# The order of keys, values and queries in the second layer's first blocks (linear attention and a Mish MLP, two layers, one core)

## The chip, the cores and the metric

One core of one Trainium2 chip runs the whole program in one launch. The metric is device time in microseconds (us). Engines: TensorE (PE in the profile, its weight loads PEld), VectorE (DVE), ScalarE (ACT), GpSimd (POOL), and SyncE (SP), which issues every data transfer (DMA) of this kernel.

## The reference

x has 2048 rows of 640. Two sublayers, A and B, alternate, each behind a layer norm and with a residual; the pair is run twice with the same weights.

```
x = x + A(layernorm(x)); x = x + B(layernorm(x)); x = x + A(layernorm(x)); x = x + B(layernorm(x))

A: q, k, v = split(x @ wqkv) into 32 heads of 20
   pq = q @ w_phi[h];  pk = k @ w_phi[h]
   phi = concat(softmax(p), softmax(-p))          # 40 features a head, for q and for k
   kv = phi_k^T v;  z = sum of phi_k over the rows
   o = (phi_q kv) / (phi_q z + 1e-6);  return o @ wo
B: h = x @ w1 + b1;  return (h * tanh(softplus(h))) @ w2      # 640 -> 1536 -> 640
```

All is float32. The products of A's keys with its values run over all 2048 rows before any query can be answered.

## The kernel before

**Precision.** Each float32 operand of a large product is kept as a high and a low part in a faster matmul type, and a product is three matmuls (high x high, high x low, low x high). So a projection of 128 rows to 640 columns is 2 halves x 5 chunks of the depth x 3 = 30 matmuls of 128x320 (`project_half`, L344).

**Stages of a layer.** `attend_first` projects keys, values and queries and sums keys times values; `attend_second` answers the queries and applies wo; `dense` is B. Rows go in 8 blocks of 256, each two tiles of 128 rows. The matmuls of B's second product are L733, of its first L691.

**`attend_first`.** For each block there are six units, a letter and a tile number: k0, k1, v0, v1, q0, q1. A unit is a projection (30 matmuls), an eviction by ScalarE (`act`, L116) and, for keys and queries, the feature chain in `features`: two reductions (L368), two subtractions (L369 and L371; for queries L369 is on POOL), an exponential on ScalarE, a sum (L377), a reciprocal (L378) and a scaling on POOL (L379). Keys then multiply their values into one accumulator, kva (L416, 32 small matmuls a tile). Queries are transposed on VectorE (L424) and stored (L428). Units are generators: `pending` holds the running ones, and `advance` moves each a step on after every new unit's projection has been recorded.

The projections read the block's rows as transposed chunks, xth (high) and xtl (low, made on VectorE, L286): two chunks of 128x512 and one of 128x256. In the second layer the rows of the next block are loaded already transposed (L325), and its chunks are made while the present block is recorded (`nxt.step()`).

**On-chip accumulators.** Projections use the "mm" ring (two tiles of two banks). The values of block 0 use the "one" ring instead (four banks, L436), which also holds kva (one bank, from its memset L484 to the stage's end) and B's first product. While B's last contraction still holds both "mm" tiles, the values of block 0 can already run.

**Weights.** In the first layer the queries' and keys' weights are folded with w_phi and spilled to `wp_d`. In the second they come back: `load_q_weights` (L179, ten loads of 320 KB into the "r2" buffers, which held B's second weights), `load_k_weights` (L185, ten into "r1", which held B's first weights). The values' weights are loaded raw (L126) and split by ScalarE (L127) and VectorE (L128) in `load_v_weights`, inside `dense`. wo's rows are loaded (L141) and split by ScalarE (L148) and POOL (L149) after block 1 has been recorded (`load_o_weights`).

**What sets the order.** The stage stands in a block whose instructions a scheduler orders by the readiness that it estimates; the recorded order decides between instructions that are ready together. ScalarE's `act` operations keep the recorded order. Only `attend_second`'s TensorE and SP orders are written by hand.

Of the kernel before, what the change touches and what calls it, by code (L numbers as in the profile page):

```python
# [41 lines left out]
def kernel(  # L42
# [118 lines left out]
    def r2_pair(j):  # L161
        if j >= 10:
            w = r2_wide(j)
            return w[:, 0], w[:, 1]
        return tuple(wts.tile([P, D], F32R, tag=f"r2{s}{j}", name=f"r2{s}{j}") for s in "hl")
# [9 lines left out]
    def load_q_weights():  # L175
        ws = [r2_pair(k) for k in range(KD)]
        for k in range(KD):
            for s in range(2):
                nc.sync.dma_start(ws[k][s].bitcast(F32), wp_d[0, s, k])  # L179
        return ws  # L180

    def load_k_weights(kv_ws):
        for k in range(KD):
            for s in range(2):
                nc.sync.dma_start(kv_ws[k][s][:, :D].bitcast(F32), wp_d[1, s, k])  # L185
# [69 lines left out]
    def norm_scale(b, mvs):  # L255

        ve = work.tile([P, BT], F32, tag="ve", name="ve", bufs=2)
        for t in range(BT):
            nc.gpsimd.tensor_scalar(ve[:, t:t + 1], mvs[t][:, 1:2], LN_EPS, 1.0, op0=ALU.add, op1=ALU.mult)
        nc.gpsimd.tensor_tensor(stats[:, b, 0], ve, neg_half, op=ALU.pow)  # L260
        for t in range(BT):
            nc.vector.scalar_tensor_tensor(stats[:, b, 1, t:t + 1], mvs[t][:, 0:1], -1.0,
                                           stats[:, b, 0, t:t + 1], op0=ALU.mult, op1=ALU.mult)
# [55 lines left out]
    def load_turned(src, tiles):  # L319

        cols = []
        for c, make in zip(range(0, KD, 2), tiles):
            n = min(2, KD - c)
            cols.append(make()[:, :n * BLK].rearrange("p (k s) -> p k s", k=n))
            nc.sync.dma_start(cols[-1], src[c * P:(c + n) * P].rearrange("(k p) s -> p k s", p=P))  # L325
        return Transposed(cols=cols)
# [55 lines left out]
    def fetch(x_src, b, xt=None):  # L382
        xt = x_tile() if xt is None else xt
        nc.sync.dma_start(xt, row_block(x_src, b))
        return xt

    def attend_first(layer, x_src, first):


        def fetch_normed(b):  # L390
            if layer:
                return load_turned(n2_d[b], [row_tile] * 3)
            xt = fetch(x_src, b)
            norm_scale(b, [norm_stats(t, xt) for t in range(BT)])
            return xt

        pending = []

        def advance():
            for g in pending[::-1]:  # L400
                try:
                    next(g)
                except StopIteration:
                    pending.remove(g)

        def keys(xts, i, v):
            e = big_tile()
            yield from features(project(xts, i % BT, kv_ws, 0), e, False)
            yield
            if i % BT == 0 and BT < i < NT - BT:  # L410
                yield
            for r in range(9):
                for j in range(4):
                    h = 3 * (4 * (r // 3) + j) + r % 3
                    if h < H:
                        nc.tensor.matmul(kva[32 * j:32 * j + DH + 1, 40 * r:40 * r + 40],  # L416
                                         v[:, (DH + 1) * h:(DH + 1) * (h + 1)], e[:, 40 * h:40 * h + 40],
                                         start=(i == 0 and r == 0), stop=(i == NT - 1), skip_group_check=True)

        def queries(xts, i, ps=None):  # L420
            e = query_tile(i)
            yield from features(project(xts, i % BT, q_ws, 0) if ps is None else ps, e, True)

            nc.vector.transpose(e, e)  # L424
            b, t = divmod(i, BT)
            dst = e_d[b].rearrange("(j f) (t q s) -> t q f j s", f=32, t=BT, s=32)
            for q in range(4):
                nc.sync.dma_start(dst[t, q], e[32 * q:32 * q + 32].rearrange("f (j s) -> f j s", s=32))  # L428
                if b == NB - 1:
                    yield  # L430

        def values(xts, i, v):
            vv = v.rearrange("p (h d) -> p h d", d=DH + 1)
            act(vv[:, :, DH], ident[:, :H], AF.Copy, scale=0.0, bias=1.0)
            if i < BT:
                pv = project(xts, i, kv_ws, D, [one_tile(), one_tile()])  # L436
                for c in range(2):
                    act(vv[:, c * H // 2:(c + 1) * H // 2, :DH],
                        pv[c][:, :HC].rearrange("p (h d) -> p h d", d=DH), AF.Copy)
            else:  # L440
                pv = project(xts, i % BT, kv_ws, D)
                act(vv[:, :, :DH].rearrange("p (c h) d -> p c h d", c=2),
                    both(pv).rearrange("p c (h d) -> p c h d", d=DH), AF.Copy)
            yield

        if first is None:
            with tc.manual_schedule(engines={mybir.EngineType.SP}):
                bd = big_tile()[:120, :720].rearrange("p (t c) -> p t c", t=6)
                nc.sync.dma_start(bd[:, :3], phi_bd[:, :3])
                raw = load_raw(0, range(3))  # L450
                xt = fetch_normed(0)
                nc.sync.dma_start(bd[:, 3:], phi_bd[:, 3:])
                raw += load_raw(0, range(3, 6))
                nxt = normed(0, xt).all()
                q_ws = [r2_pair(k) for k in range(KD)]
                fold_phi(q_ws, bd, raw)
                kv_ws = load_v_weights()
                raw = load_raw(1)
            nc.sync.dma_start(mask, bass.AP(tensor=head_mask.tensor, offset=head_mask.offset,
                                            ap=[[1, 120], [120 * (DH + 1), 3]]))  # L460
        else:
            nxt, kv_ws = first
            q_ws = load_q_weights()
        for b in range(NB):
            xts = nxt
            order = ("k0", "k1", "v0", "v1", "q0", "q1")
            if b == 0:
                order = ("v0", "q0", "v1", "k0", "q1", "k1")
            elif b == 1:
                order = ("k0", "q0", "k1", "v0", "q1", "v1")  # L470
            elif b == NB - 1:
                order = ("k0", "k1", "v0", "v1", "q0")
            vs = [v_tile() for _ in range(BT)]
            for n, (kind, t) in enumerate(order):
                t = int(t)
                i = b * BT + t
                if b == 0 and n == 1:
                    if layer:
                        load_k_weights(kv_ws)
                if b == 0 and n == 3:  # L480
                    if layer == 0:
                        fold_phi(kv_ws, bd, raw)
                    kva = one_tile()
                    nc.vector.memset(kva[:, :360], 0.0)  # L484
                if b == NB - 1 and n == 3:
                    loaded = {0: load(0)}
                if b + 1 < NB:
                    if n == 0:
                        xt = fetch_normed(b + 1)
                    elif n == 2:  # L490
                        nxt = xt if layer else normed(b + 1, xt)
                    elif n > 2:
                        nxt.step()
                g = {"k": lambda: keys(xts, i, vs[t]), "q": lambda: queries(xts, i),
                     "v": lambda: values(xts, i, vs[t])}[kind]()
                next(g)
                advance()
                pending.append(g)
            if b == 1:
                if layer == 0:  # L500
                    spill_qk_weights(kv_ws, q_ws)
                o_ws = load_o_weights()

        def rest():

            ps = [one_tile(), one_tile()]
            project_half(ps[0], xts, 1, q_ws, 0, 0)
            advance()
            advance()
            yield  # L510
            project_half(ps[1], xts, 1, q_ws, 0, 1, range(3))
            yield
            project_half(ps[1], xts, 1, q_ws, 0, 1, range(3, KD))
            pending.append(queries(xts, NT - 1, ps))
            next(pending[-1])
            while pending:
                yield
                advance()

        return kva, o_ws, loaded, rest()  # L520
# [374 lines left out]
```

## Time and profile before

| | us |
|---|---|
| median of 3 runs | 1383.88 (1383.01 to 1385.57) |
| the profiled execution | 1385.02 |
| its span, first to last instruction | 1383.2 |
| second layer's `attend_first` in it | about 702 to 936 |
| TensorE busy | 1364.8 |
| VectorE busy | 1082.0 |
| ScalarE busy | 583.1 |
| POOL busy | 440.5 |

The granted TensorE clock is 0.999 of full speed. A row of the time-ordered view reads: start (us from the span's start), duration, engine, line, operation, what it writes <- what it reads, shapes, count, and in brackets the engine's idle time before it with what ended that. A line's "DMA to landing" row is the time from issue to landing.

### The profile page before, as it was taken

What the parts mean: (1) busy time and instruction counts of PE and PEld (TensorE: products, weight loads), DVE (VectorE), ACT (ScalarE), POOL (GpSimd) and SP (SyncE); (2) the same over time, 40 slices, a digit from 0 to 9 for tenths busy, and PEclk for the clock granted to TensorE, in tenths of its full rate; (3) what the DMA queues carried; (4) which work ended last, traced back from release to release, by engine and by line L of the source; (5) the groups of instructions that cost most, each with busy time, mean ns of one, the idle gap of its engine ahead of it and who ended that gap; (6) DMA issues with size and microseconds to landing.
All of it is one profiled execution on the core that took longest, in us unless ns stands there. A gap on an engine that the chain in (4) does not pass through costs nothing. (4 is left out here: it accounts for less than half of the span.)

```text
span 1383.2 us, 30808 instructions
## 1 busy us (share of the span) xinstructions
PE 1364.8 (99%) x12866; PEld 1351.4 (98%) x12866; DVE 1082.0 (78%) x1820; ACT 583.1 (42%) x971; POOL 440.5 (32%) x334
## 2 busy tenths in 40 slices
PE   8999999999999999999999899999999999999998
PEld 7999999999999999999999899999999999999998
DVE  5799977886698887788769988988678776677775
ACT  4444434222445454545444333432235444444443
POOL 1353543353322222222234434453342111111112
PEclk9999999999999999999999999999999999999999
DMA  8532433779624432344474333458975211333200
GB/s 320 172 73 59 73 50 69 216 228 305 223 66 96 115 97 62 74 113 96 134 249 84 76 63 59 69 115 262 278 260 172 77 45 52 97 96 96 76 21 19
DMA packets 350276, 169.67 MB, mean 123 GB/s; under 512 B 287097, under 2 KB 323689, under 8 KB 350137
## 3 DMA queue, kind: packets, MB, share of 16 engines
q1 hardware_dynamic: 350137, 167.72, 45.0%
q8 instruction: 100, 1.64, 0.5%
q14 instruction: 39, 0.32, 0.1%
HBM read 104.76 MB, written 62.91 MB: 121 GB/s over the span
## 5 line engine op out<-in xcount | busy, mean ns | idle before, releaser
L733 PE MATMUL mm<-r2h,ol 128*128 128x320 f32 x1280 | 305.1, 309 | 0.8 <-ACT ol L716 0.8
L717 POOL TENSOR_TENSOR ol<-big,ol 128x512 fp32r<-128x512 f32 (+1 forms) x98 | 130.0, 1327 | 485.4 <-ACT ol L716 409.1
L691 PE MATMUL one<-xtl,r1h 128*128 128x256 f32 x960 | 268.2, 279 | 0.0
L691 PE MATMUL one<-xth,r1l 128*128 128x256 f32 x960 | 268.0, 279 | 0.0
L691 PE MATMUL one<-xth,r1h 128*128 128x256 f32 x960 | 265.9, 279 | 0.0
L733 PEld LDWEIGHTS mm<-r2h,ol 128*128 128x128 f32 x1280 | 219.1, 188 | 1.3 <-ACT ol L716 1.1
L733 PE MATMUL mm<-r2l,ol 128*128 128x320 f32 x640 | 197.3, 309 | 0.0
L344 PE MATMUL mm<-r1h,xtl 128*128 128x320 f32 x600 | 185.8, 310 | 1.7 <-DVE xtl L286 1.7
L344 PE MATMUL mm<-r1h,xth 128*128 128x320 f32 x600 | 187.4, 312 | 0.0
L344 PE MATMUL mm<-r1l,xth 128*128 128x320 f32 x600 | 186.0, 310 | 0.0
L691 PEld LDWEIGHTS one<-xtl,r1h 128*128 128x128 f32 x960 | 180.4, 188 | 0.0
L691 PEld LDWEIGHTS one<-xth,r1l 128*128 128x128 f32 x960 | 180.4, 188 | 0.0
L691 PEld LDWEIGHTS one<-xth,r1h 128*128 128x128 f32 x960 | 179.6, 188 | 0.0
L706 DVE TENSOR_SCALAR big<-big 128x512 f32<-128x512 f32 (+1 forms) x98 | 57.0, 582 | 109.9 <-ACT big L704 109.7
L379 POOL TENSOR_TENSOR r<-r,r 128x1280 f32<-128x1280 f32 x32 | 75.8, 2370 | 149.4 <-DVE r L378 143.5
L733 PEld LDWEIGHTS mm<-r2l,ol 128*128 128x128 f32 x640 | 120.2, 188 | 0.0
L708 ACT ACTIVATE big<-big,two 128x512 f32<-128x512 f32 (+1 forms) x98 | 70.2, 717 | 116.0 <-DVE big L707 116.0
L704 ACT ACTIVATE big<-one,b1s 128x256 f32<-128x256 f32 x192 | 80.9, 468 | 90.1 <-PE one L691 89.5
L716 ACT ACTIVATE ol<-big 128x512 fp32r<-128x512 f32 (+1 forms) x98 | 61.0, 622 | 136.3 <-DVE big L715 136.2
L344 PEld LDWEIGHTS mm<-r1h,xtl 128*128 128x128 f32 x600 | 112.7, 188 | 2.2 <-DVE xtl L286 2.1
L344 PEld LDWEIGHTS mm<-r1h,xth 128*128 128x128 f32 x600 | 112.7, 188 | 0.7
L344 PEld LDWEIGHTS mm<-r1l,xth 128*128 128x128 f32 x600 | 112.7, 188 | 0.1
(128 smaller groups left out, 3129.8 us busy)
## 6 DMA issues: line engine op xcount, KB each, us to landing
e_d<-r SPq DMA_DIRECT2D x128, 160.0 KB, 4.0
big<-e_d SPq DMA_DIRECT2D x32, 640.0 KB, 7.9
x_d<-xt SPq DMA_DIRECT2D x23, 640.0 KB, 3.7
xt<-x_d SPq DMA_DIRECT2D x22, 640.0 KB, 5.2
n_d<-xn SPq DMA_DIRECT2D x176, 80.0 KB, 2.2
xt<-in_x SPq DMA_DIRECT2D x16, 640.0 KB, 6.6
xn<-x_d SPq DMA_DIRECT2D x28, 320.0 KB, 4.7
v<-n_d SPq DMA_DIRECT2D x30, 256.0 KB, 3.1
```

Of the source, the lines that this page charges most:

```text
L344: nc.tensor.matmul(ps[:, :HC], a[:, sl], r, start=(k == 0 and n == 0), stop=(k == KD - 1 and n == 2))
L379: nc.gpsimd.tensor_tensor(eg, eg, r.unsqueeze(2).to_broadcast([P, 2 * H, DH]), op=ALU.mult)
L691: nc.tensor.matmul(ph[:, j, :], l, r, start=(n == 0), stop=(n == 3 * KD - 1))
L704: exps[0] = nc.scalar.activation(part(ta, 0)[:, j - js.start], ph[:, j, :], AF.Exp, bias=b1s[:, 2 * pr + j:2 * pr + j + 1]).ins
L706: nc.vector.tensor_scalar_min(e, e, E_CAP)
L708: nc.scalar.activation(r, n, AF.Ln, bias=two)
L716: nc.scalar.activation(ah[:, js], n, AF.Copy)
L717: nc.gpsimd.tensor_tensor(al[:, js], n, ah[:, js].bitcast(F32), op=ALU.subtract)
L733: nc.tensor.matmul(pys[t][:, c, :HC], l[:, j, sl], r, start=(f == 0 and n == 0), stop=(f == KF - 1 and n == 2))
```

## The change

```diff
             nxt, kv_ws = first
+            load_k_weights(kv_ws)
             q_ws = load_q_weights()
         for b in range(NB):
             xts = nxt
             order = ("k0", "k1", "v0", "v1", "q0", "q1")
-            if b == 0:
+            if b == 0 and layer:
+                order = ("v0", "k0", "k1", "v1", "q0", "q1")
+            elif b == 0:
                 order = ("v0", "q0", "v1", "k0", "q1", "k1")
-            elif b == 1:
+            elif b == 1 and not layer:
                 order = ("k0", "q0", "k1", "v0", "q1", "v1")
...
-                if b == 0 and n == 1:
-                    if layer:
-                        load_k_weights(kv_ws)
-                if b == 0 and n == 3:
+                if b == 0 and n == (1 if layer else 3):
                     if layer == 0:
                         fold_phi(kv_ws, bd, raw)
                     kva = one_tile()
```

Only the second layer changes. Its block 0 takes v0 k0 k1 v1 q0 q1, its block 1 the order of the later blocks. The ten loads of the keys' weights are recorded ahead of the ten of the queries'; kva is allocated and cleared after one unit of block 0 in place of three.

The two built programs, TensorE's order around the change (matmuls; L733 and values are mixed in the first entry):

```
before  v0 (30) and 20 of v1 among the last L733 | q0 30 | 10 of v1 | k0 30 | q1 30 | k1 30
        block 1: k0 30 | q0 30 | k1 30 | v0 9, L416 32, v0 21 | q1 30 | v1 30
        block 2: L416 64 | k0 30 | k1 30 | L416 32 | v0 30 | v1 30 | q0 30 | q1 30
after   v0 (30) and 15 of v1 among the last L733 | k0 30 | k1 30 | 15 of v1 | q0 30 | q1 30
        block 1: k0 14, L416 10, k0 16 | L416 22 | k1 30 | L416 32 | v0 30 | v1 30 | q0 30 | q1 30
        block 2: L416 32 | k0 30 | L416 32 | k1 30 | v0 30 | v1 30 | q0 30 | q1 30
```

## The prediction

> **What bounds the kernel now.** I read the page's head first, then the busy time by windows, then the waits of TensorE, and last the instructions in order of time around each wait that is left.
>
> ```profile
> span 1383.2 us, 30808 instructions
> PE 1364.8 (99%) x12866; PEld 1351.4 (98%) x12866; DVE 1082.0 (78%) x1820; ACT 583.1 (42%) x971; POOL 440.5 (32%) x334
> ```
>
> TensorE is busy in 99% of the span, and the change neither adds nor removes a matmul. So only TensorE's holes can pay. By windows (us; then the busy time of PE, PEld, DVE, ACT, POOL) two stretches near the start of the second layer have holes:
>
> ```profile
> 700.00:710.00 10.00, 9.17 (x61) 8.67 (x60) 5.40 (x12) 4.20 (x10) 2.64 (x2) 1.00 0.89 336
> 760.00:770.00 10.00, 5.97 (x157) 5.32 (x156) 10.00 (x10) 2.99 (x5) 5.02 (x4) 1.00 0.25 61
> ```
>
> In 760:770 TensorE is idle for 4.03 us while VectorE is full: VectorE bounds that stretch. The waits of TensorE in 690:800 name three causes (total, times, longest):
>
> ```profile
> PE one L416 <- POOL big L379: 2.8, 1, 2.8
> PE mm L344 <- DVE xtl L286: 1.3, 1, 1.3
> PE mm L733 <- ACT ol L716: 0.8, 1, 0.8
> ```
>
> The same by instruction:
>
> ```profile
> 761.14 0.83 PE L416 MATMUL one<-big,v 128*21 128x40 f32 x64
> 764.72 0.83 PE L416 MATMUL one<-big,v 128*21 128x40 f32 x64 [2.75 <-POOL big L379]
> 765.48 0.41 PE L344 MATMUL mm<-r1h,xth 128*128 128x320 f32 x1
> 765.73 0.31 PE L344 MATMUL mm<-r1l,xth 128*128 128x320 f32 x1
> ...
> 767.49 0.31 PE L344 MATMUL mm<-r1l,xth 128*128 128x320 f32 x1
> 769.08 0.42 PE L344 MATMUL mm<-r1h,xtl 128*128 128x320 f32 x1 [1.28 <-DVE xtl L286]
> 769.33 0.31 PE L344 MATMUL mm<-r1h,xth 128*128 128x320 f32 x1
> ```
>
> From 765.73 to 767.49 there are 12 projection matmuls, one per 0.147 us; the 0.31 is a record's length, so an idle time counted from it is too short. By starts: 64 records of L416 take 764.72 to 765.48, 0.76 us, so the second group could have started at 761.90; it started 2.82 us later. The low part at 769.08 could have started at 767.64, was 1.44 late, and restarted 0.10 slow (0.25 to the next). **Together 4.4 us.** The first loss is the wait for the normalised key features of block 1's first tile (L379), the second for block 2's last transposed chunk (L286). Why VectorE is late:
>
> ```profile
> 727.88 0.81 DVE L369 TENSOR_TENSOR big<-big,m 128x640 f32<-128x640 f32 x1
> 758.33 2.99 DVE L369 TENSOR_TENSOR big<-big,m 128x640 f32<-128x640 f32 x1
> 762.38 2.84 DVE L286 TENSOR_TENSOR xtl<-xn,xth 128x512 fp32r<-128x512 f32 x1
> 758.00 2.63 POOL L379 TENSOR_TENSOR big<-big,r 128x1280 f32<-128x1280 f32 x1 [5.83 <-DVE r L378]
> 761.92 2.75 POOL L379 TENSOR_TENSOR big<-big,r 128x1280 f32<-128x1280 f32 x1 [1.29 <-DVE r L378]
> ```
>
> L369 takes 0.81 alone, 2.99 when it meets POOL's L379 (758.00 to 760.63): it ends 0.69 after POOL does. So VectorE is in arrears from the features of blocks 0 and 1 alone, which for keys and queries start all at once.
>
> **The change part by part.**
>
> *Order of the six units.* Block 0 goes from v0 q0 v1 k0 q1 k1 to v0 k0 k1 v1 q0 q1, block 1 from k0 q0 k1 v0 q1 v1 to k0 k1 v0 v1 q0 q1. Each unit is 30 matmuls, and the same 12 units run before block 2. What moves is which feature chains stand first on VectorE. In the new program's VectorE order, block 1's two key chains are finished before block 2's chunks need VectorE, and the two L416 products of block 1 stand after all of block 1's projections, the second behind block 2's first.
>
> I price that by chaining the new order by hand from these rows:
>
> ```profile
> 723.04 1.55 DVE L368 TENSOR_REDUCE m<-r 128x32 f32<-128x640 f32 x2
> 728.61 1.48 DVE L377 TENSOR_REDUCE r<-r 128x64 f32<-128x1280 f32 x1
> 731.34 0.54 DVE L378 RECIPROCAL r<-r 128x64 f32<-128x64 f32 x1
> 723.94 1.28 POOL L369 TENSOR_TENSOR r<-r,m 128x640 f32<-128x640 f32 x1 [2.25 <-DVE m L368]
> 721.68 0.74 ACT L116 ACTIVATE v<-one 128x320 f32<-128x320 f32 x2
> ```
>
> Started back to back, each record but the first overlaps by some 0.08: a pair of L368 costs 1.45, L369 or L371 0.74, L377 1.40, L378 0.46, L286 0.6 (0.34 for the small one).
> - First key tile, from about 723.9: pair, L369, pair, L371, L286, L369, L377, L371, L286, L378 are 8.9, so 732.8; L379 2.37 more: 735.2. TensorE asks for it 14 matmuls into block 1, at about 737. Slack 1.8.
> - Block 1's last chunk: 732.8 + 1.45 + 1.40 = 735.6, where it meets POOL's L369 of the first query tile (735.2 + 1.28 = 736.5), so about 736.8; asked for at 737.1 behind ten L416. Slack 0.3, the smallest.
> - Block 1's first keys: from 736.5 three pairs, six L369/L371, three L377, three L378, a transpose (L424, 1.45), L286: 16.4, and 4 to 5 for meetings with POOL as above: 757.4; L379: 759.8. Asked for at about 762.6. Slack 2.8.
> - Block 1's second keys end near 763.5, asked for near 767.5; block 2's last chunk near 763.9, asked for at 765.4.
>
> So both losses go: **-4.4**, and next late is block 1's last chunk, still in time.
>
> *What the new order costs early.* v0's two banks, kva and v1's first half fill the ring of four "one" banks, so v1's second half can't run beside the last contraction as it does now.
>
> ```profile
> 707.57 0.31 PE L733 MATMUL mm<-r2h,ol 128*128 128x320 f32 x1
> 708.71 0.41 PE L733 MATMUL mm<-r2h,ol 128*128 128x320 f32 x1 [0.83 <-ACT ol L716]
> 709.25 0.31 PE L733 MATMUL mm<-r2l,ol 128*128 128x320 f32 x1
> 709.53 0.56 PE L733 MATMUL mm<-r2h,ol 128*128 128x320 f32 x2
> 708.24 0.42 ACT L716 ACTIVATE ol<-big 128x256 fp32r<-128x256 f32 x1 [1.69 <-DVE big L715]
> 709.08 1.56 ACT L127 ACTIVATE r1h<-v 128x640 fp32r<-128x640 f32 x2 [0.42 <-DMA v<-in_wv]
> ```
>
> Ahead of the wait that ends at 708.71 stand 24 value matmuls now and 18 in the new order. Its end is ScalarE's (708.24 + 0.42), not TensorE's, so the six come later for nothing: 6 x 0.147 = **+0.9**. Then four L733 (to 709.40), and the next three value matmuls need weight chunk 2, which ScalarE copies in half of 1.56 from 709.08, to 709.85: 0.45 and a slow restart 0.10. The little wait at 709.53 (0.13 + 0.10) is covered by that. **+0.3**. Bounds for this last term: -0.2, if the chunk's load is earlier, and 0.6.
>
> *More visits of L416.* Blocks 0 and 1 enter it five times instead of three. The steady chain of work prices a visit:
>
> ```profile
> 800.46 26.60 PE mm L344 x180
> 827.06 1.41 PE one L416 x126
> ```
>
> 180 matmuls at 0.147 are 26.4, shown as 26.60: 0.2 for changing over and back. Two more visits: **+0.4** (0 to 0.4).
>
> *Keys' weights ahead of queries'.* In the built order of SP's queue nothing moves: the ten query loads still stand ahead of the ten key loads, since their buffers come free earlier. The price is zero, but k0 now wants the keys' weights sooner. Key loads:
>
> ```profile
> L185 SPq DMA_DIRECT2D r1l<-wp_d x5: 320/383/629, 694.5 to 701.7; - x5
> DMA to landing us min/median/max: 4.4/6.6/8.0
> ```
>
> The last is issued at 701.7 and lands by 709.7 at the worst; k0 starts near 715. It hides behind the value matmuls with 5 us to spare; without that cover it would cost TensorE's wait one for one.
>
> *The memset of kva and the queries' stores.* L484 (0.36 now at 722.6) moves up to where VectorE waits, -0.3 of its queue, counted in the first chain. The queries' four stores per tile move behind block 3's row loads on SP; they are read back after the last block, so nothing waits for them but the next query tile's eviction (a rival below).
>
> **The sum.** -4.4 + 0.9 + 0.3 + 0.4 = -2.8. The profiled execution took 1385.02 (span 1383.2, 1.8 outside it) and would take 1382.2. It stands 1.1 over the median of 1383.88; against that the forecast is **1381.1**. The bounds of the terms: 4.0 (by windows) to 4.4 gained, 0.7 to 1.9 lost, so 1380.2 to 1381.8.
>
> **A rule of the skill against the change.** L369's 2.99 above against 0.81 is a meeting with POOL. The Trainium skill, "SBUF — State Buffer", section "SBUF: two separate sides", has a VectorE instruction with two inputs from SBUF and a GpSimd instruction share one pair of ports, exclusively, for the whole instruction. By that rule the new order isn't safe where a chunk follows a reciprocal that has just released L379; its result is the second rival.
>
> **Rivals.**
> 1. *The early loss is hidden as well.* VectorE and ScalarE have holes at 703 to 709, and if the weights' load lands sooner the three terms of +0.9, +0.3, +0.4 shrink to 0.4 together: 1383.88 - 4.4 + 0.4 = **1379.9**. For it: none of it is a long wait. Against it: 708.24 is ScalarE's own start.
> 2. *The wait comes back on a transposed chunk.* Block 1's last has 0.3 of slack, since by the lock its 0.34 waits for POOL's 1.28. If the first key tile starts 1.0 late, TensorE stalls 0.7 there, and a like delay at block 2's chunk (slack 1.5, a meeting with L379 2.37 long) costs 0.9: 1381.1 + 1.6 = **1382.7**. For it: today's wait of 1.3 is on just such a chunk. Against it: after block 1's projections VectorE has 2.8 us in hand for the keys.
> 3. *Slower: ScalarE's queue holds the bank ring.* v1's second half needs the bank that the first value eviction frees (721.68 + 0.37 today). Ahead of it on ScalarE stand the copies of wo's rows (L148), two of which wait for loads in series:
>
> ```profile
> 713.81 1.52 ACT L148 ACTIVATE r2h<-raw 128x640 fp32r<-128x640 f32 x2 [2.33 <-DMA raw<-in_wo]
> 719.28 0.74 ACT L148 ACTIVATE r2h<-raw 128x640 fp32r<-128x640 f32 x1 [3.95 <-DMA raw<-in_wo]
> DMA to landing us min/median/max: 2.9/3.0/3.3
> ```
>
> (The last row is for these loads.) The last L733 ends 0.8 later by the early loss, so the bank is free at 722.8; TensorE asks for it after k0 and k1, at 723.9. Past 1.1 us of further delay TensorE stalls one for one; were both loads as slow as the keys' slowest (8.0), 10 us late, the stall would be 8.9: **1390.0**. It is slower than before from 3.9 us of delay. Against it: 3.3 at most today, and the queue is the same. The Trainium skill, "TensorE: Matmul & The Clock Gate", section on the array's architectural detail, says that ScalarE's queue is strictly first in, first out; the 3.95 idle before the last L148 with ready value tiles behind it agrees.
>
> That the change does nothing of what it says holds only for the weights' half, by the built order.
>
> **Chances.** Forecast 0.60, rival 1 0.18, rival 2 0.15, rival 3 0.07. The line of faster by over 0.2% (about what a measurement here can tell from no change) is 1381.1, the forecast itself: I put 0.37 of its 0.60 under it, since its bounds reach 0.9 below and 0.7 above and the idle time by starts leaves out short gaps. So faster 0.37 + 0.18 = 0.55, same 0.23 + 0.15 = 0.38, slower 0.07. The range holds forecast and rivals 1 and 2, with about half a microsecond for how the median of a few runs falls (1383.01 to 1385.57 before): 1379.2 to 1383.3.
>
> **What would show it.** Right: in the new profile TensorE's waits on L379 and on xtl between 730 and 800 are gone, the one on ol (L716) has grown from 0.8 to about 1.7, a new one on r1h (L127) of some 0.3 to 0.5 stands at 709.5, and block 2's first projection starts about 2.8 us earlier in the span. Wrong: a wait on xtl near 737 (rival 2), on v's eviction near 724 (rival 3), on the queries' stores near 765, or no growth at 708 (rival 1). A change of the loads' order on SP would upset all of it, as these terms stand on their landing times.

## The result

| | before | after |
|---|---|---|
| median of 14 runs each (us) | 1383.93 (1381.83 to 1385.57) | 1382.28 (1380.81 to 1384.81) |
| the profiled execution | 1385.02 | 1381.04 |
| its span | 1383.2 | 1379.0 |

The ratio is 0.9985, 95% interval 0.9978 to 0.9992: faster by 0.15%, 2.1 us by the ratio (1.1 to 3.0), 1.65 us by the medians. That lies within the 0.2% which a measurement of this kernel can tell from no change, though no change at all lies outside the interval. Forecast were 1381.1 us and 2.8 us of gain. The two profiled executions differ by 4.0 us, twice the measured gain; where the other half comes from is the subject of what follows.

The head of the page of the changed kernel. TensorE's work is the same to 0.5 us, the span is 4.2 shorter:

```profile
span 1379.0 us, 30804 instructions
PE 1364.3 (99%) x12866; PEld 1350.7 (98%) x12866; DVE 1077.0 (78%) x1820; ACT 583.3 (42%) x971; POOL 441.0 (32%) x334
```

The changed kernel by windows (busy time of PE, PEld, DVE, ACT, POOL, then clock, DMA share, GB/s). In 760:770 TensorE is full and VectorE, which was, is no longer; in 700:710 TensorE has 0.15 more work than before and still 0.68 of holes:

```profile
700.00:710.00 10.00, 9.32 (x62) 8.80 (x61) 7.08 (x15) 5.19 (x11) 3.05 (x2) 1.00 0.84 319
760.00:770.00 10.00, 10.00 (x185) 9.49 (x185) 7.84 (x11) 2.66 (x4) 5.07 (x3) 1.00 0.50 100
```

TensorE's waits in 690:850 of the changed kernel (total, times, longest). These two are all: the ones on L379 and xtl are gone.

```profile
PE one L344 <- ACT r1h L127: 0.3, 1, 0.3
PE mm L733 <- ACT ol L716: 0.3, 1, 0.3
```

TensorE in order of time around them, changed kernel. By starts, the L733 behind 706.50 could have begun at 706.65 and began at 707.15, 0.50 late; the next values could have begun at 707.84 and began at 708.35, 0.51 late:

```profile
706.50 0.31 PE L733 MATMUL mm<-r2h,ol 128*128 128x320 f32 x1
707.15 0.41 PE L733 MATMUL mm<-r2h,ol 128*128 128x320 f32 x1 [0.33 <-ACT ol L716]
707.40 0.31 PE L733 MATMUL mm<-r2l,ol 128*128 128x320 f32 x1
707.54 0.31 PE L733 MATMUL mm<-r2h,ol 128*128 128x320 f32 x1
707.69 0.31 PE L733 MATMUL mm<-r2l,ol 128*128 128x320 f32 x1
708.35 0.71 PE L344 MATMUL one<-r1h,xth 128*128 128x320 f32 x3 [0.34 <-ACT r1h L127]
```

ScalarE at the same place, changed kernel. The copy into ol that TensorE waits for starts at 706.68; ahead of it on ScalarE and VectorE stands the split of the values' last weight chunk, for whose load (in_wv) ScalarE sat idle 2.21 us:

```profile
704.25 0.74 ACT L127 ACTIVATE r1h<-big 128x640 fp32r<-128x640 f32 x1 [2.21 <-DMA big<-in_wv]
706.68 0.42 ACT L716 ACTIVATE ol<-big 128x256 fp32r<-128x256 f32 x1 [1.69 <-DVE big L715]
707.55 1.54 ACT L127 ACTIVATE r1h<-v 128x640 fp32r<-128x640 f32 x2 [0.46 <-DMA v<-in_wv]
```

**A common zero.** TensorE, VectorE, ScalarE and POOL run the same instructions in both programs up to the last matmul of the first layer's first product (L691), yet that matmul starts at 695.28 in the profile of before and at 695.10 in that of after; over all the executions profiled here it lies between 694.45 and 697.25. So I count the second layer from that start. Block 1, block 2 and block 3 stand for the start of their first projection; the labels are those of the experiments below (before_again and before_third are the kernel before, after_again and after_third the changed one). A split starts 0.02 us after its load's landing, other than in copies_before and copies_first, where it is moved behind another copy; the loads landed there at 9.40 and 9.73.

| us after the last L691 | split of the last weight chunk starts | block 1 | block 2 | block 3 | wait on L379 |
|---|---|---|---|---|---|
| before, shown with the prediction | 10.53 | 38.41 | 70.20 | 99.21 | 2.8 |
| before_third | 10.07 | 37.93 | 69.68 | 98.69 | 2.7 |
| before_again | 9.07 | 37.07 | 67.78 | 96.79 | 1.7 |
| loads_only | 9.26 | 37.14 | 67.93 | 96.93 | 1.7 |
| copies_before | 10.07 | 37.07 | 67.39 | 96.40 | 1.3 |
| after | 9.15 | 38.29 | 67.78 | 95.25 | none |
| after_third | 9.41 | 38.50 | 68.00 | 95.46 | none |
| after_again | 9.64 | 38.72 | 68.22 | 95.69 | none |
| block1_only | 9.14 | 37.07 | 67.37 | 94.84 | none |
| kva_late | 9.37 | 37.25 | 66.79 | 94.26 | none |
| copies_first | 10.49 | 38.11 | 67.60 | 95.07 | none |

From block 3 to the end of the last projection it is 141.89 in before and 141.88 in after: all of the change's effect is ahead of block 3. Two things can be read from it. At the same landing of the weights (9.07 against 9.15) block 1 starts 1.22 later in the new order. And from block 1 to block 3 the new order takes 56.96, 56.96 and 56.97, whatever the landing, but the old one takes 60.80 and 60.76 in two profiles and 59.72 in the third. The kernel before has two forms, 1.1 us apart.

### The profile page after: what moved, and what is told of

The parts are those of the page before. It is cut to its first block, busy times and chain, and to the rows that moved or that the text cites. A ratio compares the mean times of both kernels' runs of the same rounds, so it can differ in the third digit from the quotient of the medians.

```text
span 1379.0 us, 30804 instructions
## 1 busy us (share of the span) xinstructions
PE 1364.3 (99%) x12866; PEld 1350.7 (98%) x12866; DVE 1077.0 (78%) x1820; ACT 583.3 (42%) x971; POOL 441.0 (32%) x334
## 4 chain that ended last, share of the span: by engine, by line
PE 94%; DVE 2%; DMA 1%; issue 1%; POOL 0%; SPq 0%; ACT 0%; DVEq 0%; POOLq 0%; ACTq 0%
PE mm L344 26%; PE one L691 24%; PE mm L733 24%; PE one L344 12%; PE mm L569 3%; PE one L280 2%; PE one L416 2%; PE mm L237 1%; DMA raw<-in_wqk_t 1%; DVE m L368 1%; PE one L237 0%; DMA v<-in_wv 0%; DVE big L371 0%; DVE r L377 0%; DMA raw<-in_wo 0%
## 5 line engine op out<-in xcount | busy, mean ns | idle before, releaser
L733 PE MATMUL mm<-r2h,ol 128*128 128x320 f32 x1280 | 305.0, 309 | 0.3 <-ACT ol L716 0.3
L691 PE MATMUL one<-xtl,r1h 128*128 128x256 f32 x960 | 268.2, 279 | 0.0
L691 PE MATMUL one<-xth,r1l 128*128 128x256 f32 x960 | 268.0, 279 | 0.0
L691 PE MATMUL one<-xth,r1h 128*128 128x256 f32 x960 | 265.9, 279 | 0.0
L733 PEld LDWEIGHTS mm<-r2h,ol 128*128 128x128 f32 x1280 | 219.2, 188 | 0.6 <-ACT ol L716 0.6
L733 PE MATMUL mm<-r2l,ol 128*128 128x320 f32 x640 | 197.3, 309 | 0.0
L691 PEld LDWEIGHTS one<-xtl,r1h 128*128 128x128 f32 x960 | 180.4, 188 | 0.0
L691 PEld LDWEIGHTS one<-xth,r1l 128*128 128x128 f32 x960 | 180.4, 188 | 0.0
L691 PEld LDWEIGHTS one<-xth,r1h 128*128 128x128 f32 x960 | 179.6, 188 | 0.0
L379 POOL TENSOR_TENSOR r<-r,r 128x1280 f32<-128x1280 f32 x32 | 76.6, 2395 | 154.3 <-DVE r L378 148.5
L733 PEld LDWEIGHTS mm<-r2l,ol 128*128 128x128 f32 x640 | 120.2, 188 | 0.0
L716 ACT ACTIVATE ol<-big 128x512 fp32r<-128x512 f32 (+1 forms) x98 | 61.0, 623 | 136.3 <-DVE big L715 136.2
```

Source lines behind the costliest of these rows:

```text
L379: nc.gpsimd.tensor_tensor(eg, eg, r.unsqueeze(2).to_broadcast([P, 2 * H, DH]), op=ALU.mult)
L691: nc.tensor.matmul(ph[:, j, :], l, r, start=(n == 0), stop=(n == 3 * KD - 1))
L716: nc.scalar.activation(ah[:, js], n, AF.Copy)
L733: nc.tensor.matmul(pys[t][:, c, :HC], l[:, j, sl], r, start=(f == 0 and n == 0), stop=(f == KF - 1 and n == 2))
```

## Experiments

**1. The kernel before again** (no edit).

> The kernel before, unchanged, for a second profile. Theory: the four waits of the first profile come again with the same sizes, L379 2.8, xtl 1.3, ol 0.8, and the stretch from the first layer's last L691 to the second layer's first L569 takes 241.3 us. Rival (the stretch depends on when the values' weights land): it differs by 1 us or more from 241.3, with the wait on ol changed by as much.

It took 1384.64 us, span 1382.9. TensorE's waits in 690:850 of this execution:

```profile
PE one L416 <- POOL big L379: 1.7, 1, 1.7
PE mm L344 <- DVE xtl L286: 1.3, 1, 1.3
```

No wait on ol, and the one on L379 shorter by 1.1 than in the profile that I predicted from. So the expected equal sizes did not come; the rival's difference did.

**2. A third profile of the kernel before** (no edit).

> A third profile of the kernel before. Theory (the size of the wait on L379 follows the landing of weight chunk 4): with the split at +9.1 to +9.5 us after the last first-product matmul, L379 1.5 to 2 us, no wait on ol, 238.7 to 239.5 us from there to the second part of the layer; with the split at +10.5, L379 2.8, ol 0.8, 241.3. Rival (the first profile was an outlier for another cause): no relation, 239 at any landing.

1384.96 us, span 1383.2; TensorE's waits in 690:850:

```profile
PE one L416 <- POOL big L379: 2.7, 1, 2.7
PE mm L344 <- DVE xtl L286: 1.3, 1, 1.3
PE mm L733 <- ACT ol L716: 0.4, 1, 0.4
```

It fits the theory in size, with the split at 10.07: 2.7, and 240.81 us from the last L691 to the second part of the layer, against 241.33 and 238.89 in the other two. But the relation is a step and not a slope, which the theory had not said. Setting the three executions beside each other, VectorE's instructions in this stretch have the same durations to some 0.05 us until one L369. VectorE and POOL at that place, first profile of before:

```profile
739.57 2.02 DVE L369 TENSOR_TENSOR big<-big,m 128x640 f32<-128x640 f32 x1
...
739.33 1.58 POOL L149 TENSOR_TENSOR r2l<-xn,r2h 128x640 fp32r<-128x640 f32 x1 [3.52 <-ACT r2h L148]
```

The same two in before_third:

```profile
739.67 2.05 DVE L369 TENSOR_TENSOR big<-big,m 128x640 f32<-128x640 f32 x1
...
739.45 1.58 POOL L149 TENSOR_TENSOR r2l<-xn,r2h 128x640 fp32r<-128x640 f32 x1 [3.54 <-ACT r2h L148]
```

And in before_again:

```profile
739.62 0.81 DVE L369 TENSOR_TENSOR big<-big,m 128x640 f32<-128x640 f32 x1
...
739.85 2.03 POOL L149 TENSOR_TENSOR r2l<-xn,r2h 128x640 fp32r<-128x640 f32 x1 [3.99 <-ACT r2h L148]
```

Where POOL's L149 (the low part of a row tile of wo) starts 0.24 or 0.22 ahead of VectorE's L369, L369 takes 2.02 or 2.05 and ends 0.68 or 0.69 after POOL does. Where L369 is 0.23 ahead, it takes 0.81 and POOL's instruction is the longer one, 2.03. VectorE has no slack up to block 2, so the 1.2 us go on into the wait on L379 (2.8 and 2.7 against 1.7). The Trainium skill, "SBUF — State Buffer", section "SBUF: two separate sides", has the engine that starts first hold the shared ports for its whole instruction while the other blocks; both forms agree with it, with 0.23 us deciding over 1.2. (In copies_before the two starts lie 0.02 us apart, POOL's first by the records, and VectorE's takes 0.81: starts as close as that can't be ordered by the records.) L149 starts when ScalarE has copied the same rows (L148), and that copy waits for their load. Copy and waits in the first profile and in before_again:

```profile
738.51 0.74 ACT L148 ACTIVATE r2h<-xn 128x640 fp32r<-128x640 f32 x1 [2.76 <-DMA xn<-in_wo]
```

```profile
739.03 0.74 ACT L148 ACTIVATE r2h<-xn 128x640 fp32r<-128x640 f32 x1 [3.28 <-DMA xn<-in_wo]
```

So it is a race between the landing of a wo load and VectorE's chain, whose start follows the landing of a wv load. Of the four profiles of the old order with nothing moved in it but loads, two lost it (before, before_third) and two won it (before_again, loads_only). How often the timed runs lose it can't be seen, since they have no trace.

**3. The changed kernel again, twice** (no edit).

> The changed kernel again, for a second profile. Theory: no wait on L379 and none on xtl between 730 and 850; the stretch from the first layer's last L691 to the second layer's first L569 within 0.7 us of 237.4, moving with the landing of the values' weight chunk 4 against the last L691. Rival (the gain was luck): a wait on xtl near 737, and a stretch above 238.5.

> A third profile of the changed kernel. Theory: with the split at +9.1 to +9.6, ol 0.3 to 0.8, r1h 0.3, 237.3 to 237.9 us in the stretch; with the split at +10.5, ol 1.7 and r1h 0.3, 239. Rival (no relation to the landing): 237.5 at any landing.

1381.16 and 1381.30 us. Their waits on ol are 0.8 and 0.6, on r1h 0.3 and 0.3, with the split at 9.64 and 9.41: ol follows the landing, as expected of them (0.3 at 9.15, 0.6 at 9.41, 0.8 at 9.64), and block 1 moves with it (38.29, 38.50, 38.72). From there on the three are equal, and the race of experiment 2 is gone. After:

```profile
738.23 1.86 POOL L369 TENSOR_TENSOR r<-r,m 128x640 f32<-128x640 f32 x1
740.05 1.57 POOL L149 TENSOR_TENSOR r2l<-xn,r2h 128x640 fp32r<-128x640 f32 x1
...
740.12 2.18 DVE L371 TENSOR_TENSOR r<-m,r 128x640 f32<-128x640 f32 x1 [1.17 <-POOL r L369]
```

L149 here follows a subtraction of POOL's own without a gap, more than 1 us after ScalarE's copy was done (738.95), so its start doesn't hang on the load. VectorE's L371 meets it in all three profiles (2.18, 2.20, 2.19), and TensorE doesn't wait for that: the new order meets L149 every time and loses nothing by it, as the keys behind it are ready 3.2 us ahead of their use (shown below). A split at 10.5, where I expected a wait of 1.7, did not occur.

**4. Only the loads' order**, on the kernel before:

```diff
             nxt, kv_ws = first
+            load_k_weights(kv_ws)
             q_ws = load_q_weights()
...
-                if b == 0 and n == 1:
-                    if layer:
-                        load_k_weights(kv_ws)
                 if b == 0 and n == 3:
```

> Only the keys' ten loads recorded ahead of the queries' ten; the order of the units and kva as before. Theory: the built order of every engine is that of before, so 1383.9, within 0.1%, and TensorE's waits on L379 (2.8) and xtl (1.3) stay. Rival (the loads' place is worth something): faster by 0.5 us or more, with r1h landing earlier.

1384.72 us, ratio 1.0000 (0.9991 to 1.0008). This part of the change is worth nothing that can be measured, and its profile is that of before in its better form (1.7 on L379, not the 2.8 that was expected).

**5. Only block 1's order**, on the kernel before:

```diff
-            elif b == 1:
+            elif b == 1 and not layer:
                 order = ("k0", "q0", "k1", "v0", "q1", "v1")
```

> The order of the later blocks in block 1 alone; block 0 and the weights' loads as before. Theory: most of the loss of 4.4 us on L379 and xtl goes (two waits of about 1.1 each stay, near 757), and none of the early cost comes (TensorE's wait on ol, L716, stays 0.8, none on r1h): faster than before by about 1.9 us, 1382.0. Rival (the gain comes from block 0's early keys): no gain, L379 and xtl still cost 4 us.

1382.54 us, ratio 0.9986 (0.9976 to 0.9995): the gain of the whole change. Of the two waits of about 1.1 that were expected, one is left in 690:850:

```profile
PE mm L344 <- ACT v L116: 0.9, 1, 0.9
```

Without block 0's new order the 1.22 us at the start aren't paid (block 1 at 37.07). In return 0.9 is lost on an eviction of values that the full change doesn't wait for (37.07 to 94.84 is 57.77, against 56.96). The two come to the same within half a microsecond, 94.84 and 95.25.

**6. Only block 0's order and the loads**, the changed kernel with block 1 put back:

```diff
-            elif b == 1 and not layer:
+            elif b == 1:
                 order = ("k0", "q0", "k1", "v0", "q1", "v1")
```

> The new order in the second layer's block 0 alone; block 1 stays k0 q0 k1 v0 q1 v1. Theory (the order of the feature chains decides which wait VectorE ends late): both halves of the order are needed. The queries' chains of block 0 now stand last, so their stores end late, and block 1's q0, still second, needs the same query tile: TensorE stalls by several us on a query's eviction between 750 and 785. Chained by hand: 8 and 7 us there, slower than before by about 13 us (1397). Rival (the gain of the change is early keys in block 0, whatever block 1 does): faster by 2 us, no wait on L379.

1401.24 us, ratio 1.0121 (1.0105 to 1.0136), slower by some 16 us, where 13 were expected. TensorE's waits in 690:850 of it, then ScalarE's row at the end of the longest:

```profile
PE mm L344 <- ACT r L116: 16.8, 2, 9.5
PE mm L733 <- ACT ol L716: 0.7, 1, 0.7
PE one L344 <- ACT r1h L127: 0.3, 1, 0.3
```

```profile
757.68 0.70 ACT L116 ACTIVATE r<-mm 128x640 f32<-128x640 f32 x1 [16.50 <-DMA e_d<-r]
```

With q0 and q1 at the end of block 0 and q0 second in block 1, a query tile's eviction into r wants a buffer that still holds an earlier query tile's features, and sits 16.50 us until their store (e_d<-r) has read it. The projections then stand for want of the banks. Block 0's new order needs block 1's: it ends on the queries, and the old block 1 has one unit (k0) before the next query tile, the new one four, behind which the stores are done.

**7. kva taken up later**, the changed kernel with its bank claimed after four units of block 0 and not after one:

```diff
-                if b == 0 and n == (1 if layer else 3):
+                if b == 0 and n == (4 if layer else 3):
```

> The changed kernel, but kva is taken and cleared after four units of block 0 (n == 4), so that v1 gets both its banks at once and all 40 early value matmuls run beside the last contraction again. Theory (the new order costs 0.9 us early for the six value matmuls that come later, and some for r1h): TensorE's waits on ol (L716) and r1h (L127) are as in the kernel before (none or one below 0.8, by the landing of the values' weights), about 1.2 us faster than the changed kernel, some 2.8 us faster than before. Rival (the early loss was bad luck of one execution): the same time as the changed kernel within 0.5 us.

1380.72 us, ratio 0.9975 (0.9963 to 0.9987). v1 has its two banks again: as in the kernel before, 24 value matmuls stand among the last L733 ahead of the wait on ol (18 in the changed kernel), 26 follow right behind, and v1's last ten come after k1. In 690:850 its profile has no wait of TensorE at all. Block 1 starts at 37.25 in place of 38.50 at the same landing (9.37 and 9.41): 1.25 us, the price of the early loss as a whole.

**8. The split of three weight chunks (ScalarE's copy and VectorE's low part) behind the last copy into ol**, on the changed kernel (its lines from 128 on are one higher, from 680 on two):

```diff
-    def split(hi, lo, src, stage):
+    def split(hi, lo, src, stage, after=None):
...
-        nc.scalar.activation(hi, st, AF.Copy)
-        nc.vector.tensor_tensor(lo, st, hi.bitcast(F32), op=ALU.subtract)
+        with tc.issue_after(after) if after is not None else ExitStack():
+            nc.scalar.activation(hi, st, AF.Copy)
+            nc.vector.tensor_tensor(lo, st, hi.bitcast(F32), op=ALU.subtract)
...
-                  (row_tile, row_tile, v_tile, v_tile, big_tile)[k])
+                  (row_tile, row_tile, v_tile, v_tile, big_tile)[k], after if k > 1 else None)
...
-            nc.scalar.activation(ah[:, js], n, AF.Copy)
+            copies[0] = nc.scalar.activation(ah[:, js], n, AF.Copy).ins
...
-                    kv_ws = load_v_weights()
+                    kv_ws = load_v_weights(copies[0])
```

> The changed kernel, but the splits of the values' weight chunks 2 to 4 (L127, L128) are issued behind the last activation copy (L716) on ScalarE and VectorE, not ahead of it. Theory (TensorE's wait on ol ends when the load of chunk 4 has landed, since its split stands ahead of L714, L715 and L716): the wait on ol goes, the wait on r1h grows by part of it, 0.3 to 0.6 us faster than the changed kernel. Rival (ol is late by the activation's own chain): the wait stays.

1380.31 us, ratio 0.9969 (0.9957 to 0.9981). ScalarE in this kernel (L718 is L716, L128 is L127): the copy into ol now stands ahead of the last chunk's and waits for no load.

```profile
705.51 0.42 ACT L718 ACTIVATE ol<-big 128x256 fp32r<-128x256 f32 x1 [3.23 <-DVE big L717]
705.83 0.72 ACT L128 ACTIVATE r1h<-big 128x640 fp32r<-128x640 f32 x1
708.38 1.57 ACT L128 ACTIVATE r1h<-v 128x640 fp32r<-128x640 f32 x2 [1.83 <-DMA v<-in_wv]
```

TensorE's waits in 690:850 of it:

```profile
PE one L345 <- ACT r1h L128: 0.4, 1, 0.4
PE one L345 <- DVE r1l L129: 0.2, 1, 0.2
```

The wait on ol is gone. The last chunk's load landed at 9.73 after the last L691, later than in after_again (9.61, wait 0.8), and the copy into ol started at 10.17 instead of 12.06: that it hung on the split ahead of it is shown by this edit. The wait on r1h stays, as that one is for the load of another chunk. By its median this kernel is 2.0 us ahead of the changed one (six executions, in another series of runs), where 0.3 to 0.6 was expected and the table has 0.2 to 0.6 at block 3; where the rest comes from is open.

**9. Experiments 7 and 8 together.**

> kva taken late and the splits behind the last copy. Theory: neither wait on ol nor on r1h above 0.3, no wait on L379 or xtl up to 850, 1.2 to 1.6 us faster than the changed kernel, some 3 us faster than before. Rival: not faster than kva taken late alone, since with 24 value matmuls ahead ol is in time anyway where the load lands early.

1380.93 us, ratio 0.9976 (0.9966 to 0.9986), no better than either alone. Its profile, the slowest of its eight executions, reaches block 3 at 94.19 and has no wait in 690:850, but a later one of 1.3 us on a key tile's scaling (L380 there, L379 in the changed kernel). Among these three the runs can't tell.

**10. The splits' move with the old order, and with block 1's order alone.** Edit as in 8, on the kernel before and on experiment 5's.

> The kernel before with the copies of the values' weight chunks 2 to 4 (L128 here, L127 before) put behind the last copy of the hidden activations (L716 before). Theory: in the kernel before, the split of chunk 4 stands ahead of that copy, so the start of the feature chains hangs on a load that lands 9.1 to 10.5 us after the last first-product matmul, but an early landing leaves TensorE no wait on ol (none in the second profile of before), and VectorE's chains still start together: a gain of 0 to 1.5 us, about 1383.2; the waits on L379 and xtl stay, 1.5 to 3 us together. Rival (the copies' place is worth the 2.2 us that it gave with the new order in whatever order the units are): 1381.7, and the waits on L379 and xtl fall under 1 us.

> Block 1's new order alone, with the same move of the three copies. Theory: block 1's order alone shows no wait on ol or r1h, only 0.9 us for a value eviction, so the copies' move has little to remove: 1382.5, within 0.7 of block 1's order alone, and the wait of 0.9 on the eviction stays. Rival (the move is worth 2.2 us in every order): 1380.3.

1383.49 us, ratio 0.9997 (0.9989 to 1.0006), and 1382.69 us, ratio 0.9989 (0.9980 to 0.9998). So the move is worth nothing measurable where TensorE asks for ol late; the rival, 2.2 us in every order, falls twice. The old order keeps its two waits, and block 1's order alone keeps its 0.9 on the eviction. In the profile of copies_before TensorE waits in 690:850 for (L380 is L379 there, L287 L286):

```profile
PE one L417 <- POOL big L380: 1.3, 1, 1.3
PE mm L345 <- DVE xtl L287: 1.3, 1, 1.3
```

## Why the prediction was right, and where its size was not

- **What bounds the kernel: right.** The two late waits came from VectorE's arrears, and block 1's order removes them (experiment 5); no matmul was added or dropped.
- **The gain of 4.4: right in the profile that it was read from, mis-sized for the kernel.** That is the term that failed. Block 1 to block 3 went from 60.80 to 56.96, 3.84, against 4.4 - 0.4 = 4.0 with the visits. But 1.1 of it was L369's meeting with L149, lost in that execution. In before_again the same two waits are, by starts, 1.73 and 1.54, together 3.3 and not 4.4, and block 1 to block 3 gains 2.76. I had one profile and took its wait for a property of the program. The 2.02 of that L369 was in the trace; had I asked what it met, I would have seen that 0.24 us decided.
- **Early cost of 0.9 + 0.3: right in sum.** Block 1 starts 1.22 later at the same landing, and 1.25 earlier when kva's claim is undone (experiment 7). Its parts in after are 0.50 on ol and 0.51 on r1h by starts, each with a restart slower by 0.10, which makes 1.21. So the sum came as forecast, and the misses of its two terms cancel: less on ol, more on r1h. The forecast wait of 1.7 on ol isn't there (0.3 to 0.8), because these executions' weights landed earlier; at such a landing the old order had no wait there.
- **Two more visits of L416 at 0.2: a little low, not measured alone.** 4.36 by starts less 0.4 is 3.96, where 3.84 was found; in before_again 3.27 less 0.4 is 2.87, where 2.76 was found. By these differences a visit costs 0.26.
- **The slacks: right where the trace shows them.** Of the changed kernel, POOL's scaling of the first and of block 1's first keys, VectorE's last chunk of block 1, and the matmuls that ask for them:

```profile
731.42 2.37 POOL L379 TENSOR_TENSOR big<-big,r 128x1280 f32<-128x1280 f32 x1 [10.66 <-DVE r L378]
756.52 2.37 POOL L379 TENSOR_TENSOR big<-big,r 128x1280 f32<-128x1280 f32 x1 [1.16 <-DVE r L378]
```

```profile
733.98 1.33 DVE L286 TENSOR_TENSOR xtl<-xn,xth 128x256 fp32r<-128x256 f32 x1
```

```profile
735.53 0.40 PE L416 MATMUL one<-big,v 128*21 128x40 f32 x20
735.86 0.42 PE L344 MATMUL mm<-r1h,xtl 128*128 128x320 f32 x1
...
762.12 0.83 PE L416 MATMUL one<-big,v 128*21 128x40 f32 x64
762.88 0.42 PE L344 MATMUL mm<-r1h,xth 128*128 128x320 f32 x1
```

  The first keys are ready at 733.79 and asked for at 735.53, 1.7 of slack (forecast 1.8); the last chunk at 735.31, asked for at 735.86 at the earliest, at least 0.5 (0.3); block 1's first keys at 758.89 and 762.12, 3.2 (2.8). The chunk's 1.33 is the meeting with a POOL L369 that was foreseen.
- **Loads' order at nothing: right** (experiment 4).
- **The sum.** By block 3 the new order gains 1.54 where the old one wins its race (96.79 to 95.25, weights landing alike) and 2.6 where it loses it (3.84 - 1.22, the 1.22 measured at the early landing alone). The forecast of 2.8 belongs to the second case. The measured 2.1 lies between the two; its interval, 1.1 to 3.0, excludes neither. The first two profiles differ by more (99.21 to 95.25) for a second reason: the weights landed 1.4 later in before, so block 1 starts there at 38.41 and the new order's early cost hardly shows against 38.29.
- **Rivals.** Rival 1 (early loss hidden as well): no, until kva's claim is moved. Rival 2 (a wait on a chunk): no such wait in three profiles. Rival 3 (ScalarE's queue holds the ring): no wait on a value's eviction, though ScalarE's L148 ahead of it waited for wo about as long as before (3.55, 3.80 and 4.16 us in the three profiles, 3.95 before). The side on which the prediction put most, faster by over 0.2%, did not come; the range, 1379.2 to 1383.3, holds the time.

What stays open: the profiled executions of the two kernels differ by 3.98, 3.48 and 3.66 us in the three pairs of profiles, and the medians of 14 by 1.65. Up to block 3 the table accounts for 2.76 of the mean of 3.7 (98.23 less 95.47, each the mean of three); the rest lies ahead of the common zero and behind block 3, where the change touches nothing. How many timed executions fall in which form isn't known, and the profiles needn't stand for them: the three of the changed kernel all lie below its median of 14. That the lost race makes the longer form was read from four profiles of the old order that differ there in nothing else; no edit that forces it was run. Nor can the runs rank experiments 7, 8 and 9, whose intervals overlap; each beats the changed kernel in its median, by 1.4 to 2.0 us, but in another series of runs.

## What to carry to other kernels

A wait read from one profile is one draw: ahead of pricing a change by it, look on VectorE for an instruction that takes two or three times its usual duration, ask which POOL instruction it met and what released that one; if it was a load, the wait is a matter of a few tenths and its size wants a second profile. Put executions on a common zero, the last instruction that the change can't touch, and compare stages there and not spans. And when an order is moved, ask which bank or buffer the moved unit claims: claiming kva's bank after the first unit rather than the fourth cost 1.2 of the gain, and block 0's half of the order without block 1's cost 16.

## What the runs showed of the hardware that was not expected

- The same program runs in two forms by some 0.5 us between a load's landing and VectorE's chain: 0.81 or 2.02 to 2.05 us for one VectorE subtraction, and 1.1 us by block 3.
- The split of one weight chunk, timed from the same matmul, started at 9.07, 10.07 and 10.53 us in three executions of one program; the first 695 us of identical work differ by up to 2.8 us between executions (694.45 to 697.25); the cause is open.
